# Backward of two attention blocks: every DMA on SyncE's queue, and a group's `wo` fetched head by head

## The chip, the cores and the metric

The kernel runs on one core of a Trainium2 chip. The metric is the device time of one execution in microseconds (us). The engines named below are TensorE (PE, with PEld for its weight loads), VectorE (DVE), ScalarE (ACT), GpSimd (POOL) and SyncE (SP). SyncE computes nothing here: its instruction stream is a queue of DMA issues with the semaphore waits that stand before them.

## What is computed

Two attention blocks, A and B, of the same shapes but with their own data, run forward, and then all gradients are formed for a given `grad_out`. There are 8 batches of 96 query tokens (768 rows), a model width of 640, 32 heads of width 128, and a cache of 512 keys per batch and head. Everything is bf16.

```python
q = (x @ wq) split into heads
p = softmax((q @ k_cache^T) * Dh**-0.5)
o = p @ v_cache
out = concat_heads(o) @ wo                      # for A and for B, side by side in out
# returned: out, and for both blocks dx, dk_cache, dv_cache, dwq, dwo
```

## The kernel before, in words

**Ticks.** The work is cut into items, one for each head and batch: 8 to a head, 512 in all. `build_block` gives every piece of an item, a head or a group a tick and a slot, and `Emitter.run` (L25) emits all pieces sorted by tick, then slot. Item *b* of head *h* starts at tick `tick0 + 8h + b`, and its stages follow at the ticks of `OFF` (L45): load at 0, transposes of K and V at 2, scores and exponential at 3, dV at 4, the output at 5, dP and dS at 6, dK and the transposition of dS at 7, dQ at 8. So in one tick TensorE does one stage of each of several items. The framework then schedules the emitted instructions and fixes for each engine, and for SyncE's queue, one static order. An instruction waits in that order for the semaphores of what it needs, and everything behind it on its engine waits too.

**One item on SyncE's queue.** `c_ld` (L235) loads K and V (128 KB each, 11 buffers of `K_sb` and 8 of `V_sb`); `c_s4` (L341) and `c_s7` (L407) store dV and dK (128 KB each, 6 buffers each). That is 32 issues for each head.

**One head.** `pA` (L174) loads the head's slice of `wq` as `wq_h` (one buffer, 640 runs of 256 bytes) and transposes by DMA its slice of `wo` into `woT_h` (one buffer); `pW` (L192) transposes a slice of `wq` into `wqT_h`; `pC` projects q and dO; `qA` (L410) transposes the finished `OT_h` and `dQT_h` by DMA into `Onat` and `dQnat` (one buffer each); `qB` (L419) forms dwo in two halves from `Onat` and stores it; `qD` (L437) forms dwq in three parts from `dQnat` and stores it. By `HK` (L46) `dQnat` is transposed at tick 16 after the head's first, and the matmuls that read it (L450) stand at ticks 19 to 21, three to five ticks later, which is in the stream of items of the head after the next.

**One group.** 8 heads are a group, and each block has 4. After a group's last item, `gU` (L471) sums the eight heads' products with `wo_r` (out) and with `wqT_h` (dx) in 12 units each, spread over 26 ticks (`GSPREAD`). These ticks hold more TensorE work, so they are longer. `gW` (L459) loads the whole group's `wo` into one tile `wo_r`, in a single DMA of 1280 KB.

**Which queue.** SyncE's queue has the item traffic, the DMA transposes, block A's x and g, the first `wq_h`, and block B's output rows. GpSimd issues the other `wq_h` loads, the stores of dwo and dwq, the `wo_r` loads, block A's output rows, block B's x and g in natural layout (L139) and block B's column chunks of g (L106). GpSimd also computes `P_sb` (L296) and `prod` (L350), in the same instruction stream as its DMA issues. Block B's x comes through five DMA transposes `xT` (L99) on SyncE's queue.

**Waits on SyncE's queue.** The DMAs of a queue share 8 completion semaphores in turn, and each issue waits for the landing of the DMA eight places before it, besides its own data or buffer.

Of the kernel before, what the change touches and what calls it, by code (L numbers as in the profile page):

```python
# [11 lines left out]
BF16 = mybir.dt.bfloat16  # L12
# [18 lines left out]
SL_LOAD = 0  # L31
# [10 lines left out]
SL_GRP = 95  # L42
SL_SETUP = 96

OFF = dict(ld=0, s1=2, s2=3, s3=3, s4=4, s5=5, s6=6, s7=7, s8=8)  # L45
# [3 lines left out]
GSPREAD = 26  # L49
# [3 lines left out]
def build_block(tc, em, tick0, blk, x, kc, vc, wq, wo, g_all, out_all, dx, dk, dv, dwq, dwo, ident, ones, pools, HG=8, first=True, groups=None):  # L53
    nc = tc.nc
    B, Sq, D = x.shape
# [8 lines left out]
    HG = min(HG, H)  # L64
    if groups is None:
        assert H % HG == 0
        groups = [HG] * (H // HG)
    assert sum(groups) == H and max(groups) <= HG
    NG = len(groups)
    GH0 = [sum(groups[:i]) for i in range(NG)]  # L70
# [8 lines left out]
    g_flat = g_all.rearrange("b s d -> (b s) d")[:, blk * D:(blk + 1) * D]  # L79
    out_flat = out_all.rearrange("b s d -> (b s) d")[:, blk * D:(blk + 1) * D]  # L80
    dx_flat = dx.rearrange("b s d -> (b s) d")
    wq_v = wq.rearrange("(c p) n -> p c n", p=128)
    dwq_v = dwq.rearrange("(c p) n -> p c n", p=128)

    const, ps, kvp, wk, hd, hst, grp = (pools[k] for k in ("const", "ps", "kvp", "wk", "hd", "hst", "grp"))

    def bank(shape, dt, name):
        return ps.tile(shape, dt, name=name, tag="bank")

    S = {}  # L90
    G = {}
    HS = pools["HS"]
    CS = pools["CS"]

# [7 lines left out]
    def setup_ld(c):  # L102
        def f():
            tmp = const.tile([128, TT, 128], BF16, name="ld_tmp", bufs=2)
            with nc.allow_non_contiguous_dma(reason="setup column chunk"):
                tc.keep_in_program_order(nc.gpsimd.dma_start(tmp[:], g_flat[:, c * 128:(c + 1) * 128].rearrange("(t p) d -> p t d", p=128)))  # L106
            S[("tmp", c)] = tmp
        return f

# [23 lines left out]
    def setup_nat(which_, t0=0, nt=TT):  # L133
        def f():
            key = "x_nat" if which_ == 0 else "g_nat"
            src_flat = x_flat if which_ == 0 else g_flat
            if t0 == 0:
                S[key] = const.tile([128, TT, D], BF16, name=key, bufs=1)
            (nc.sync if first else nc.gpsimd).dma_start(S[key][:, t0:t0 + nt, :],  # L139
                                                        src_flat[t0 * 128:(t0 + nt) * 128, :].rearrange("(t p) d -> p t d", p=128))  # L140
        return f

    def setup_acc():
        if NG > 1:
            S["out_acc"] = const.tile([128, TT, D], F32, name="out_acc", bufs=1)
            S["dx_acc"] = const.tile([128, TT, D], F32, name="dx_acc", bufs=1)
# [18 lines left out]
    def evac(eng, dst, src, sc=None):  # L165
        if eng == "act":
            nc.scalar.activation(dst, src, ACT.Identity, scale=(1.0 if sc is None else sc))
        else:
            if sc is None:
                nc.vector.tensor_copy(dst, src)  # L170
            else:
                nc.vector.tensor_scalar(dst, src, float(sc), None, op0=ALU.mult)

    def pA(h):  # L174
        def f():
            cols = slice(h * 128, (h + 1) * 128)
            wq_h = hd.tile([128, DC, 128], BF16, name="wq_h", bufs=1)
            with nc.allow_non_contiguous_dma(reason="per-head wq slice"):
                (nc.sync if first and h == 0 else nc.gpsimd).dma_start(wq_h[:], wq_v[:, :, cols])
            woT_h = hd.tile([128, DC, 128], BF16, name="woT_h", bufs=1)  # L180
            nc.sync.dma_start_transpose(woT_h[:], wo[cols, :])
            HS[(blk, h)] = dict(wq_h=wq_h, woT_h=woT_h)
        return f
# [235 lines left out]
    def qB(h, di):  # L419
        def f():  # L420
            st = HS[(blk, h)]
            Onat = st["Onat"]
            if "dwo_sb" not in st:
                st["dwo_sb"] = hd.tile([128, D], BF16, name="dwo_sb")
                st["dwo_n"] = 0
            dwo_sb = st["dwo_sb"]
            (c0, w) = dsplits[di]
            w_ps = bank([128, w], F32, "dwo_ps")
            for t in range(TT):
                nc.tensor.matmul(w_ps[:], Onat[:, t, :], S["g_nat"][:, t, c0:c0 + w], start=(t == 0), stop=(t == TT - 1))  # L430
            evac(EV["qB%d" % di], dwo_sb[:, c0:c0 + w], w_ps[:])
            st["dwo_n"] += 1
            if st["dwo_n"] == len(dsplits):
                nc.gpsimd.dma_start(dwo[h * 128:(h + 1) * 128, :], dwo_sb[:])
        return f

    def qD(h, c_lo, c_hi):  # L437
        def f():
            st = HS[(blk, h)]
            dQnat = st["dQnat"]  # L440
            if "dwq_sb" not in st:
                st["dwq_sb"] = hd.tile([128, DC, 128], BF16, name="dwq_sb")
                st["dwq_n"] = 0
            dwq_sb = st["dwq_sb"]
            ncn = c_hi - c_lo
            w_ps = bank([128, 4 * 128], F32, "dwq_ps")
            for ci in range(ncn):
                c = c_lo + ci
                for t in range(TT):
                    nc.tensor.matmul(w_ps[:, ci * 128:(ci + 1) * 128], S["x_nat"][:, t, c * 128:(c + 1) * 128], dQnat[:, t, :],  # L450
                                     start=(t == 0), stop=(t == TT - 1))
            evac("act" if ncn > 1 else "dve", dwq_sb[:, c_lo:c_hi, :].rearrange("p a b -> p (a b)"), w_ps[:, 0:ncn * 128])
            st["dwq_n"] += ncn
            if st["dwq_n"] == DC:
                with nc.allow_non_contiguous_dma(reason="per-head dwq slice"):
                    nc.gpsimd.dma_start(dwq_v[:, :, h * 128:(h + 1) * 128], dwq_sb[:])
        return f

    def gW(g):  # L459
        def f():  # L460
            wo_r = grp.tile([128, HG, D], BF16, name="wo_r", bufs=1)
            ld = nc.gpsimd.dma_start(wo_r[:, 0:groups[g], :], wo[GH0[g] * 128:(GH0[g] + groups[g]) * 128, :].rearrange("(h p) d -> p h d", p=128))
            tc.keep_in_program_order(ld)
            G[g] = dict(wo_r=wo_r)
            if g == 0:
                setup_acc()
        return f

# [2 lines left out]
    def gU(g, which, t, gi):  # L471
        def f():
            acc = S.get("out_acc" if which == 0 else "dx_acc")
            dst_flat = out_flat if which == 0 else dx_flat
            (c0, w) = gsplits[gi]
            o_ps = bank([128, w], F32, "o_ps")
            for hh in range(groups[g]):
                h = GH0[g] + hh
                src = HS[(blk, h)]["OT_h"] if which == 0 else HS[(blk, h)]["dQT_h"]
                rhs = G[g]["wo_r"][:, hh, c0:c0 + w] if which == 0 else HS[(blk, h)]["wqT_h"][:, c0:c0 + w]  # L480
                nc.tensor.matmul(o_ps[:], src[:, t * 128:(t + 1) * 128], rhs, start=(hh == 0), stop=(hh == groups[g] - 1))  # L481
            if NG == 1:
                ob = wk.tile([128, w], BF16, name="ob", bufs=4)
                evac(EV["gU"], ob[:], o_ps[:])
                nc.gpsimd.dma_start(dst_flat[t * 128:(t + 1) * 128, c0:c0 + w], ob[:])
            elif g == 0:
                evac(EV["gU"], acc[:, t, c0:c0 + w], o_ps[:])
            elif g < NG - 1:
                nc.vector.tensor_tensor(acc[:, t, c0:c0 + w], o_ps[:], acc[:, t, c0:c0 + w], op=ALU.add)
            else:  # L490
                ob = wk.tile([128, w], BF16, name="ob", bufs=4)
                nc.vector.tensor_tensor(ob[:], o_ps[:], acc[:, t, c0:c0 + w], op=ALU.add)
                (nc.gpsimd if first else nc.sync).dma_start(dst_flat[t * 128:(t + 1) * 128, c0:c0 + w], ob[:])
        return f

    NTS = len(tsplits)
# [2 lines left out]
    for g in range(NG):  # L499
        h0 = GH0[g]  # L500
        for hh in range(groups[g]):
            h = h0 + hh
# [32 lines left out]
            for (k_, c_lo, c_hi) in qd_parts:  # L535
                if c_lo < DC:
                    em.add(c0t + k_, SL_HEAD + 2, qD(h, c_lo, min(c_hi, DC)))
        cLg = tick0 + (h0 + groups[g] - 1) * B + B - 1
        em.add(cLg + OFF["s5"] - 2, SL_LOAD, gW(g))
        units = [(t, gi) for t in range(TT) for gi in range(len(gsplits))]  # L540
        for i, (t, gi) in enumerate(units):
            em.add(cLg + OFF["s5"] + 2 + (i * GSPREAD) // len(units), SL_GRP, gU(g, 0, t, gi))
# [116 lines left out]
```

## Time and profile before

| what | value |
|---|---|
| median of 3 runs | 1777.6 us (1771.38 to 1781.83) |
| profiled execution: its own time | 1778.72 us |
| profiled execution: span | 1776.9 us |
| granted TensorE clock, mean | 0.995 |
| busy share PE / PEld / DVE / ACT / POOL | 99 / 83 / 82 / 83 / 40 % |
| DMA time of SyncE's queue (q1), of 16 engines' span | 70.5 %, 319.82 MB |
| DMA time of GpSimd's queue (q0) | 8.8 %, 46.71 MB |
| DMA issues in the trace: SyncE / GpSimd | 2340 / 230 |

The span is the profiled part of that execution; 1.8 us of its own time lie around it. The profile is of one execution, so its parts are compared with 1778.72 us, and that time lies 1.1 us above the median of the three runs. In lines of the timeline the two first numbers are the start and the length in us; `SPq` marks an instruction of SyncE's queue, whose length is that of the issue and not that of the transfer. In lists of waits the three numbers are the total in us, how often, and the longest. Line numbers (L450) are those of the kernel before.

### The profile page before, as it was taken

Reading aid. Unit: us, or ns where it says so; the run is one execution under the profiler, and the core shown is the slowest. Engines: PE = TensorE matmul, PEld = TensorE weight load, DVE = VectorE, ACT = ScalarE, POOL = GpSimd, SP = SyncE. Lnnn points to the kernel's source line nnn. Section 1 sums busy time; section 2 is a strip of 40 time slices with the busy share of each in tenths; the row PEclk is TensorE's granted clock in tenths of the full one; section 3 lists DMA queues with packets and bytes.
Section 4 is the critical chain, followed back from the end, with each engine's and each line's share of the span. In section 5 each row is a group of like instructions: output and inputs, shape, how many; then the busy total and the mean of one; then the engine's idle time right before and its main releaser. Section 6 shows DMA issues by size and latency. Waiting matters only on the chain.

```text
span 1776.9 us, 65815 instructions
## 1 busy us (share of the span) xinstructions
PE 1752.8 (99%) x24538; PEld 1476.6 (83%) x24538; DVE 1449.4 (82%) x3106; ACT 1470.3 (83%) x4081; POOL 717.1 (40%) x1260
## 2 busy tenths in 40 slices
PE   8999899999999999999899999999999999999998
PEld 6888788888888888888788888888888888888886
DVE  7888766888878887788687888668987788878894
ACT  5999788899778987798777999789987799877992
POOL 2444433444334443345344444334443344433441
PEclk9999999999999999999899999999999999999999
DMA  8889975899858896689997799678896788867874
GB/s 212 220 221 221 240 191 167 206 217 237 210 168 214 217 245 186 178 209 223 236 254 188 211 222 248 186 178 208 221 245 183 182 219 225 238 179 174 222 215 128
DMA packets 508657, 370.73 MB, mean 209 GB/s; under 512 B 230000, under 2 KB 497136, under 8 KB 508336
## 3 DMA queue, kind: packets, MB, share of 16 engines
q1 hardware_dynamic: 493072, 319.82, 70.5%
q0 software_dynamic: 15264, 46.71, 8.8%
q8 instruction: 192, 3.15, 0.8%
q14 instruction: 129, 1.06, 0.2%
HBM read 160.10 MB, written 159.12 MB: 180 GB/s over the span
## 4 chain that ended last, share of the span: by engine, by line
PE 97%; DMA 2%; DVE 1%; issue 0%; ACT 0%; POOL 0%; SPq 0%; ACTq 0%; DVEq 0%; POOLq 0%
PE q_ps L215 12%; PE o_ps L481 12%; PE dK_ps L404 6%; PE dV_ps L338 6%; PE kvT_ps L249 6%; PE kvT_ps L251 6%; PE dP_ps L360 6%; PE S_ps L265 6%; PE dwq_ps L450 6%; PE dwo_ps L430 6%; PE dq_dst_ps L387 5%; PE optp_ps L321 5%; PE optp_ps L312 5%; PE dq_dst_ps L378 5%; PE n_ps L231 4%; DMA xT<-in_B_x_dram 1%
## 5 line engine op out<-in xcount | busy, mean ns | idle before, releaser
L296 POOL TENSOR_SCALAR P_sb<-E_sb,rinv 96x512 bf16<-96x512 bf16 x512 | 352.3, 688 | 680.6 <-DVE rinv L287 674.7
L277 ACT ACTIVATE E_sb<-S_ps,negm 96x512 bf16<-96x512 f32 x512 | 348.7, 681 | 152.1 <-DVE negm L267 151.4
L364 DVE SCALAR_TENSOR_TENSOR dS_sb<-dP_ps,dl_ps,P_sb 96x512 bf16<-96x512 f32 x512 | 384.7, 751 | 106.6 <-PE dl_ps L362 97.6
L267 DVE TENSOR_REDUCE negm<-S_ps 96x1 f32<-96x512 f32 x512 | 348.2, 680 | 56.7 <-PE S_ps L265 55.1
L253 DVE COPY KVT<-kvT_ps 128x1024 bf16<-128x1024 bf16 x512 | 348.5, 681 | 18.5 <-PE kvT_ps L251 6.3
L406 ACT ACTIVATE dK_sb<-dK_ps 128x512 bf16<-128x512 f32 x512 | 302.9, 592 | 51.9 <-PE dK_ps L404 48.5
L340 ACT ACTIVATE dV_sb<-dV_ps 128x512 bf16<-128x512 f32 x512 | 315.6, 616 | 0.0
L327 ACT ACTIVATE PT_sb<-optp_ps 128x384 bf16<-128x384 bf16 x512 | 254.3, 497 | 0.0
L350 POOL TENSOR_TENSOR prod<-OT_h,dOT_h 128x96 bf16<-128x96 bf16 x512 | 186.8, 365 | 106.4 <-ACT OT_h L324 87.4
L249 PE MATMUL kvT_ps<-ident,K_sb 128*128 128x128 bf16 x2048 | 198.4, 219 | 0.0
L251 PE MATMUL kvT_ps<-ident,V_sb 128*128 128x128 bf16 x2048 | 198.4, 219 | 0.0
L404 PE MATMUL dK_ps<-Qnat_h,dS_sb 96*128 96x128 bf16 x2048 | 198.4, 219 | 0.0
L338 PE MATMUL dV_ps<-dOnat_h,P_sb 96*128 96x128 bf16 x2048 | 198.1, 219 | 0.0
L265 PE MATMUL S_ps<-KVT,QT_h 128*96 128x512 bf16 x512 | 194.3, 380 | 1.2 <-DVE KVT L253 1.2
L360 PE MATMUL dP_ps<-KVT,dOT_h 128*96 128x512 bf16 x512 | 195.5, 382 | 0.0
L249 PEld LDWEIGHTS <-K_sb 128*128 128x128 bf16 x2048 | 152.1, 98 | 37.2 <-issue 2.0
L389 DVE COPY dST_sb<-dq_dst_ps 128x384 bf16<-128x384 bf16 x512 | 178.9, 349 | 2.1 <-PE dq_dst_ps L387 1.6
L321 PE MATMUL optp_ps<-ident,P_sb 96*128 96x96 bf16 x2048 | 171.9, 205 | 2.4 <-POOL P_sb L296 2.3
L387 PE MATMUL dq_dst_ps<-ident,dS_sb 96*128 96x96 bf16 x2048 | 172.5, 206 | 0.8 <-DVE dS_sb L364 0.4
L312 PE MATMUL optp_ps<-PT_sb,V_sb 128*128 128x96 bf16 x2048 | 172.5, 206 | 0.0
L378 PE MATMUL dq_dst_ps<-dST_sb,K_sb 128*128 128x96 bf16 x2048 | 171.1, 206 | 0.0
L450 PE MATMUL dwq_ps<-dQnat,x_nat 128*128 128x128 bf16 x1920 | 160.3, 220 | 5.0 <-DMA dQnat<-dQT_h 5.0
(71 smaller groups left out, 3560.3 us busy)
## 6 DMA issues: line engine op xcount, KB each, us to landing
out_dram<-dV_sb SPq DMA_DIRECT2D x512, 128.0 KB, 2.6
out_dram<-dK_sb SPq DMA_DIRECT2D x512, 128.0 KB, 2.6
K_sb<-in_A_k_cache_dram SPq DMA_DIRECT2D x256, 128.0 KB, 2.8
V_sb<-in_A_v_cache_dram SPq DMA_DIRECT2D x256, 128.0 KB, 2.7
K_sb<-in_B_k_cache_dram SPq DMA_DIRECT2D x256, 128.0 KB, 2.6
V_sb<-in_B_v_cache_dram SPq DMA_DIRECT2D x256, 128.0 KB, 2.6
out_dram<-dwo_sb POOLq DMA_DIRECT2D x64, 160.0 KB, 3.0
out_dram<-dwq_sb POOLq DMA_DIRECT2D x64, 160.0 KB, 3.2
```

Of the source, the lines that this page charges most:

```text
L249: nc.tensor.transpose(kvT_ps[:, c * 128:(c + 1) * 128], st["K_sb"][:, c, :], ident[:])
L251: nc.tensor.transpose(kvT_ps[:, Sk + c * 128:Sk + (c + 1) * 128], st["V_sb"][:, c, :], ident[:])
L253: nc.vector.tensor_copy(KVT[:], kvT_ps[:])
L267: nc.vector.tensor_reduce(negm[:], S_ps[:], axis=AX.X, op=ALU.max, negate=True)
L277: nc.scalar.activation(E_sb[:], st["S_ps"][:], ACT.Exp, bias=st["negm"][:], scale=1.0, accum_out=rowsum[:])
L296: nc.gpsimd.tensor_scalar(P_sb[:], st["E_sb"][:], st["rinv"][:], 0.0, op0=ALU.mult, op1=ALU.add)
L338: nc.tensor.matmul(dV_ps[:, c * 128:(c + 1) * 128], P_sb[:, c * 128:(c + 1) * 128], hs["dOnat_h"][:, b * 128:(b + 1) * 128], start=True, s ...
L340: nc.scalar.activation(dV_sb[:], dV_ps[:], ACT.Identity, scale=1.0)
L360: nc.tensor.matmul(dP_ps[:], hs["dOT_h"][:, tok], st["VT"], start=True, stop=True)
L364: nc.vector.scalar_tensor_tensor(dS_sb[:], dP_ps[:], dl_ps[:, 0:1], st["P_sb"][:], op0=ALU.subtract, op1=ALU.mult)
L404: nc.tensor.matmul(dK_ps[:, c * 128:(c + 1) * 128], dS_sb[:, c * 128:(c + 1) * 128], hs["Qnat_h"][:, b * 128:(b + 1) * 128], start=True, s ...
L406: nc.scalar.activation(dK_sb[:], dK_ps[:], ACT.Identity, scale=1.0)
```

## The change

Every `nc.gpsimd.dma_start` becomes `nc.sync.dma_start`. The single load of a group's `wo` becomes eight loads of 160 KB, one for each head, into eight tiles of their own. They stand in the last 31 ticks of the group's 64 (from tick 33 of the group on, about one every four ticks), where the single load stood two ticks before the group's last item was through its stage 5. The matmuls are the same and read the head's tile.

```diff
-                tc.keep_in_program_order(nc.gpsimd.dma_start(tmp[:], g_flat[:, c * 128:(c + 1) * 128]...
+                tc.keep_in_program_order(nc.sync.dma_start(tmp[:], g_flat[:, c * 128:(c + 1) * 128]...
...
-            (nc.sync if first else nc.gpsimd).dma_start(S[key][:, t0:t0 + nt, :],
+            nc.sync.dma_start(S[key][:, t0:t0 + nt, :],
...
-                (nc.sync if first and h == 0 else nc.gpsimd).dma_start(wq_h[:], wq_v[:, :, cols])
+                nc.sync.dma_start(wq_h[:], wq_v[:, :, cols])
...
-                nc.gpsimd.dma_start(dwo[h * 128:(h + 1) * 128, :], dwo_sb[:])
+                nc.sync.dma_start(dwo[h * 128:(h + 1) * 128, :], dwo_sb[:])
...
-                    nc.gpsimd.dma_start(dwq_v[:, :, h * 128:(h + 1) * 128], dwq_sb[:])
+                    nc.sync.dma_start(dwq_v[:, :, h * 128:(h + 1) * 128], dwq_sb[:])
...
-    def gW(g):
+    def gW(g, hh):
         def f():
-            wo_r = grp.tile([128, HG, D], BF16, name="wo_r", bufs=1)
-            ld = nc.gpsimd.dma_start(wo_r[:, 0:groups[g], :], wo[GH0[g] * 128:(GH0[g] + groups[g]) * 128, :]...
-            tc.keep_in_program_order(ld)
-            G[g] = dict(wo_r=wo_r)
-            if g == 0:
+            h = GH0[g] + hh
+            wo_r = grp.tile([128, D], BF16, name="wo_r", bufs=HG)
+            tc.keep_in_program_order(nc.sync.dma_start(wo_r[:], wo[h * 128:(h + 1) * 128, :]))
+            HS[(blk, h)]["wo_r"] = wo_r
+            if g == 0 and hh == 0:
                 setup_acc()
...
-                (nc.gpsimd if first else nc.sync).dma_start(dst_flat[t * 128:(t + 1) * 128, c0:c0 + w], ob[:])
+                nc.sync.dma_start(dst_flat[t * 128:(t + 1) * 128, c0:c0 + w], ob[:])
...
-        em.add(cLg + OFF["s5"] - 2, SL_LOAD, gW(g))
+        lead = 2 + OFF["s5"] + GSPREAD
+        for hh in range(groups[g]):
+            em.add(tick0 + h0 * B + lead + ((groups[g] * B - lead) * hh) // groups[g], SL_GRP + 2, gW(g, hh))
```

The order that the scheduler fixes for TensorE, VectorE and ScalarE is the same as before, instruction for instruction. GpSimd's order loses its 230 DMA issues. SyncE's queue goes from 2340 DMA issues to 2626.

More of the change, by code (lines that the diff above doesn't have):

```diff
@@ L90, in build_block @@
     S = {}
-    G = {}
     HS = pools["HS"]
@@ L105, in f @@
             with nc.allow_non_contiguous_dma(reason="setup column chunk"):
-                tc.keep_in_program_order(nc.gpsimd.dma_start(tmp[:], g_flat[:, c * 128:(c + 1) * 128].rearrange("(t p) d -> p t d", p=128)))
+                tc.keep_in_program_order(nc.sync.dma_start(tmp[:], g_flat[:, c * 128:(c + 1) * 128].rearrange("(t p) d -> p t d", p=128)))
             S[("tmp", c)] = tmp
@@ L455, in f @@
                 with nc.allow_non_contiguous_dma(reason="per-head dwq slice"):
-                    nc.gpsimd.dma_start(dwq_v[:, :, h * 128:(h + 1) * 128], dwq_sb[:])
+                    nc.sync.dma_start(dwq_v[:, :, h * 128:(h + 1) * 128], dwq_sb[:])
         return f
-    def gW(g):
+    def gW(g, hh):
         def f():
-            wo_r = grp.tile([128, HG, D], BF16, name="wo_r", bufs=1)
-            ld = nc.gpsimd.dma_start(wo_r[:, 0:groups[g], :], wo[GH0[g] * 128:(GH0[g] + groups[g]) * 128, :].rearrange("(h p) d -> p h d", p=128))
-            tc.keep_in_program_order(ld)
-            G[g] = dict(wo_r=wo_r)
-            if g == 0:
+            h = GH0[g] + hh
[3 more added lines that the diff above has]
+            if g == 0 and hh == 0:
                 setup_acc()
@@ L479, in f @@
                 src = HS[(blk, h)]["OT_h"] if which == 0 else HS[(blk, h)]["dQT_h"]
-                rhs = G[g]["wo_r"][:, hh, c0:c0 + w] if which == 0 else HS[(blk, h)]["wqT_h"][:, c0:c0 + w]
+                rhs = HS[(blk, h)]["wo_r"][:, c0:c0 + w] if which == 0 else HS[(blk, h)]["wqT_h"][:, c0:c0 + w]
                 nc.tensor.matmul(o_ps[:], src[:, t * 128:(t + 1) * 128], rhs, start=(hh == 0), stop=(hh == groups[g] - 1))
@@ L484, in f @@
                 evac(EV["gU"], ob[:], o_ps[:])
-                nc.gpsimd.dma_start(dst_flat[t * 128:(t + 1) * 128, c0:c0 + w], ob[:])
+                nc.sync.dma_start(dst_flat[t * 128:(t + 1) * 128, c0:c0 + w], ob[:])
             elif g == 0:
@@ L492, in f @@
                 nc.vector.tensor_tensor(ob[:], o_ps[:], acc[:, t, c0:c0 + w], op=ALU.add)
-                (nc.gpsimd if first else nc.sync).dma_start(dst_flat[t * 128:(t + 1) * 128, c0:c0 + w], ob[:])
+                nc.sync.dma_start(dst_flat[t * 128:(t + 1) * 128, c0:c0 + w], ob[:])
         return f
```

## Prediction

> **What bounds the kernel.** I read the page's first two parts, then the waits, then TensorE's few idle places in the windows view, and last the timeline of SyncE's queue. TensorE sets the end:
>
> ```profile
> PE 1752.8 (99%) x24538; PEld 1476.6 (83%) x24538; DVE 1449.4 (82%) x3106; ACT 1470.3 (83%) x4081; POOL 717.1 (40%) x1260
> ...
> DMA  8889975899858896689997799678896788867874
> ```
>
> TensorE is idle in few places, and nearly all of that is DMA:
>
> ```profile
> POOL P_sb L296 <- DVE rinv L287: 674.7, 389, 8.2
> ...
> PE q_ps L215 <- DMA xT<-in_B_x_dram: 6.3, 3, 2.7
> ...
> PE dwq_ps L450 <- DMA dQnat<-dQT_h: 5.0, 1, 5.0
> ...
> PE tp_ps L129 <- DMA x_nat<-in_A_x_dram: 4.5, 2, 3.8
> ```
>
> The 674.7 us are GpSimd's own spare time; TensorE waited 2.3 us for `P_sb` in all. So GpSimd's 230 issues cost nothing now, and taking them away frees an engine that nobody waits for. The two stalls in mid-run cost more than their length, since the granted clock falls after them (columns: window, length, busy us of PE, PEld, DVE, ACT, POOL, then PEclk, DMA share, GB/s):
>
> ```profile
> 190.00:204.00 14.00, 14.00 (x210) 11.99 (x207) 12.54 (x28) 13.13 (x38) 7.32 (x13) 1.00 1.03 199
> 204.00:214.00 10.00, 4.96 (x53) 4.44 (x51) 2.77 (x6) 3.00 (x11) 1.30 (x3) 0.66 1.03 301
> ...
> 846.00:859.00 13.00, 7.23 (x55) 5.47 (x55) 3.09 (x7) 3.38 (x9) 2.00 (x4) 0.61 0.97 252
> ```
>
> A clock of 0.66 over 10 us loses 3.4 us beside the wait of 5.0 us; 0.61 over 13 us loses 5.1 us beside 6.3 us.
>
> Now SyncE's queue, between two groups of units (start, length of the issue):
>
> ```profile
> 343.43 0.43 SPq L407 DMA_DIRECT2D out_dram<-dK_sb  x1
> 343.95 0.39 SPq L341 DMA_DIRECT2D out_dram<-dV_sb  x1
> 344.44 0.43 SPq L239 DMA_DIRECT2D K_sb<-in_A_k_cache_dram  x1
> 344.96 0.39 SPq L240 DMA_DIRECT2D V_sb<-in_A_v_cache_dram  x1
> 345.44 0.47 SPq L407 DMA_DIRECT2D out_dram<-dK_sb  x1
> 346.01 1.66 SPq L416 DMA_TRANSPOSE dQnat<-dQT_h  x1
> 347.76 0.54 SPq L341 DMA_DIRECT2D out_dram<-dV_sb  x1
> 348.39 0.38 SPq L239 DMA_DIRECT2D K_sb<-in_A_k_cache_dram  x1
> ```
>
> Each issue starts 0.1 us after the last one ended: **the queue is full**. A head is 36 issues, 32 direct and 4 transposes. From the K load at 340.2 us to the one a head later it takes 24.9 us, and the next two heads 24.5 and 25.4 us, while TensorE needs 23.84 us for a head without units. So the queue falls behind by about 1 us a head. During a group's units a head lasts 27 to 32 us, the queue has pauses of some 30 us in all, and it catches up. Whoever is served late shows it first at `dQnat`: the time from its landing to its first matmul (L450) is 8.8, 6.5, 4.6, 4.1, 2.1 us for heads 10 to 14 (of 0 to 63).
>
> **What the change does, part by part.** TensorE's, VectorE's and ScalarE's orders stay the same, so only waits can move the time.
>
> *The burst goes.* One transpose of 64 was hit by the 1280 KB load:
>
> ```profile
> 198.49 0.95 POOL L462 DMA_DIRECT2D wo_r<-in_A_wo_dram  x1
> ...
> L416 SPq DMA_TRANSPOSE dQnat<-dQT_h x64: 1217/1277/2718, 51.3 to 1745.6; - x64
> ...
> DMA to landing us min/median/max: 2.5/3.8/10.4
> ```
>
> It was issued 0.3 us after that load and took 10.4 us instead of 3.85: 6.5 us come back. The other seven loads were issued after their transpose, which landed in 2.5 to 4.8 us, so nothing comes back there.
>
> *286 issues come to SyncE's queue* (230 less the 8 big loads, plus 64 small ones). Price: a direct issue of 128 runs takes 0.38 us and 0.10 us to the next, 0.48 us. A `wq_h` issue (640 runs) stands on this queue once, at the start, with 0.47 us: 0.56 us; I give the dwq store, of the same shape, the same. The mean, 0.52 us, is my price. From below: 0.43 us (0.33 us, an issue after a pause, and 0.10). From above: behind that one `wq_h` the next transpose took 2.79 us against 1.24 us; if half the new issues each held up the queue by 1.5 us more, the mean is 1.3 us. I take the near row, because six other loads of 256 runs stood in front of that transpose too.
>
> *Where they stand.* In heads with units three a head come in, in heads without units five (`wq_h`, dwo, dwq and two of `wo_r`, whose eight loads fall into the last 31 ticks of the group, where the queue is full). Counted in the new order, from the queue's last pause to the last `dQnat` before a group's units (heads 6, 14, 22, 29, 38, 46, 54, 62), against the time to spare of that `dQnat`:
>
> | group | added | x 0.52 us | to spare | new wait of TensorE |
> |---|---|---|---|---|
> | 1 | 27 | 14.0 | -5.0 + 6.5 | 12.5 |
> | 2 | 19 | 9.9 | 2.1 | 7.8 |
> | 3 | 19 | 9.9 | 4.8 | 5.1 |
> | 4 (setup of B) | 14 | 7.3 | 4.9 | 2.4 |
> | 5 | 25 | 13.0 | 3.2 | 9.8 |
> | 6 | 19 | 9.9 | 2.9 | 7.0 |
> | 7 | 19 | 9.9 | 6.3 | 3.6 |
> | 8 | 18 | 9.4 | 7.9 | 1.5 |
>
> Sum 49.7 us, less the 5.0 us already waited: **+44.7 us**. The waits come in pieces at the `dQnat` of two to four heads; behind L450 in TensorE's order stands all of the next items' work, so each piece delays everything. In the units' heads the queue has some 30 us of pauses against 8 us of new issues and up to 13 us of lateness, so that is made good there and each group starts anew. The K and V loads have 1 to 3 us more to spare at most in those heads and would be the next to be late.
>
> *Setup of B.* `xT` waits already now. Before its last chunk 17 issues are added (8.8 us, 2.4 of them already counted), and behind it come two more `ld_tmp` (1.0 us): **+7.4 us**.
>
> *Block A's output rows, B's x and g in natural layout*: 26 issues in heads with units, hidden by the queue's pauses there; without that cover 26 x 0.52 = 13.5 us.
>
> *Clock.* In the two rows above a stall costs 0.7 to 0.8 us of clock per us waited. Taken on all 52 us this would be +37; but a TensorE at half clock also gives the queue that time, so it replaces the next wait and only the last of a stretch counts. Ends: -8.5 (the two old losses vanish) and +28 (37 less 8.5, which are in the span). I take **+5**, nearer to none, as the pieces are short.
>
> **Sum:** 1778.7 + 44.7 + 7.4 + 5 = **1836 us**, 57 us over the profiled execution and 3.3% over the median of 1777.6 us.
>
> **Two rules that speak against this.** The queue of rows above is full at 0.48 us an issue. The Trainium skill, "DMA: Bandwidth & Descriptors", section "Issuing engines are not separate DMA queues", says that DMAs issued from several engines run on the same 16 DMA engines, and spreading them saves only issue time, "usually small relative to the DMA itself". By that rule the sum is without the issue terms, the profiled execution less the stall at 204 us and its clock loss, near 1770 us. Here an issue is short against its landing (0.4 against 2.6 us), but 36 of them fill a head.
>
> On the clock: gaps of 2.74, 2.04 and 1.52 us within 7.2 us led to the 0.61 row. The skill's "TensorE: Matmul & The Clock Gate", section "Part 1: The HAM clock gate", has the clock halve after an idle window of about 3.4 us; by that alone no piece under 3.4 us costs clock, and the clock term would be near -8.5 instead of +5.
>
> **Rivals.**
> 1. *The queue has room, the burst was the problem* (ends on the other side). Then the stall at 204 us goes with its clock loss, 5.0 + 3.4 us: 1770 us; if `xT` also lands in time without GpSimd's traffic, 11.4 us more: 1759 us. For it: the worst stall is the burst's. Against it: no pause in four heads of SyncE's queue. It decides if 19 issues cost less than 2.1 to 6.3 us, 0.1 to 0.3 us each.
> 2. *Partly absorbed*: at the low price of 0.43 us the eight waits are 35.5 us, setup 5, clock -8.5: 35.5 - 5.0 + 5 - 8.5 = +27, 1806 us; if loads also land faster, down to 1787.
> 3. *The 256-byte runs are dear.* At 1.3 us an issue, 19 issues are 25 us and the eight waits 174 us: with 20 us in the setup 1973 us at the far end; at 0.8 us they are 94 us, setup 12: 1778.7 + 94 - 5.0 + 12 + 5 = 1885 us. For it: the 2.79 us, and the DMA engines are already at 0.95 to 1.03 in these heads. Against: one row only, at the start.
>
> **Chances.** Forecast (1806 to 1865) 0.55; rival 3 (above 1865) 0.17; rival 2's lower part (1787 to 1806) 0.11; no change 0.08; rival 1 below 1769 us 0.09. What this measurement can tell from no change is about 0.5%, 1768.7 to 1786.5 us. So faster 0.09, same 0.08, slower 0.83. The range 1788 to 1892 us leaves out those two and a few hundredths above.
>
> **What would show it.** Right: waits `PE dwq_ps L450 <- DMA dQnat` of 30 to 70 us in 15 to 30 pieces, at the ends of groups; SyncE's heads without units at 26.5 to 27.5 us; no pauses there; rows of PEclk below 1.00 near the stalls; GpSimd waiting for nothing new. Wrong: SyncE's issues of `wq_h` or dwq far from 0.47 us, transposes behind them over 2 us, the K and V loads as the main releaser of TensorE, or `dQnat` landing in under 3 us throughout.

## The result, and the profile after

| what | before | after |
|---|---|---|
| median of the runs beside each other | 1778.8 us (4 runs) | 1833.53 us (4 runs, 1827.56 to 1837.91) |
| ratio to before | | 1.0312, 95% interval 1.0268 to 1.0356 |
| profiled execution: its own time / span | 1778.72 / 1776.9 us | 1827.56 / 1825.7 us |
| TensorE idle between its first and its last matmul | 17.0 us | 52.6 us |
| SyncE's queue, a head without units | 24.54 us for 36 issues | 27.30 us for 41 issues |

The change costs 3.1%; forecast were 1836 us. The last row is the mean over the 22 heads that have no units in them and exactly these numbers of issues, their time taken from one head's first K load to the next. In the lines below the numbers of the lines are one lower than before (L450 is now L449), since the change takes a line out near the top.

First the page of after, its lines of the engines, of the DMA engines' busy tenths and of SyncE's queue:

```profile
PE 1766.2 (97%) x24538; PEld 1481.0 (81%) x24538; DVE 1449.9 (79%) x3106; ACT 1469.6 (80%) x4081; POOL 539.9 (30%) x1030
...
DMA  7888886889867887778887877977778777887774
...
q1 hardware_dynamic: 603760, 366.53, 77.6%
```

GpSimd is busy 177 us less and nobody gains by it. The DMA engines are no fuller than before: the bytes are the same, and one queue now has nearly all of them. Next, what TensorE waited for (total, times, longest):

```profile
PE dwq_ps L449 <- DMA dQnat<-dQT_h: 23.6, 16, 3.3
PE kvT_ps L248 <- DMA K_sb<-in_A_k_cache_dram: 7.4, 5, 3.7
PE kvT_ps L250 <- DMA V_sb<-in_A_v_cache_dram: 5.8, 10, 1.5
PE kvT_ps L250 <- DMA V_sb<-in_B_v_cache_dram: 5.8, 9, 1.3
...
PE tp_ps L116 <- DMA ld_tmp<-in_grad_out_dram: 4.5, 1, 4.5
...
PE kvT_ps L248 <- DMA K_sb<-in_B_k_cache_dram: 0.6, 1, 0.6
```

The `dQnat` wait that before had once, for 5.0 us, is there 16 times. K and V, for which TensorE never waited, take 19.6 us in 25 pieces. The `xT` row of before (6.3 us) is gone, and `ld_tmp` has come in its place. So the readers of four different DMAs wait a little each, and what these four have in common is the queue.

The windows view, for the two places shown of before and for four new ones (busy us of PE, PEld, DVE, ACT, POOL, then PEclk, DMA share, GB/s):

```profile
190.00:204.00 14.00, 12.82 (x201) 11.02 (x199) 11.04 (x26) 11.79 (x35) 4.21 (x9) 1.00 0.86 226
204.00:214.00 10.00, 10.00 (x138) 8.21 (x137) 9.05 (x20) 9.37 (x28) 4.19 (x8) 1.00 0.75 204
133.00:139.00 6.00, 3.19 (x52) 2.76 (x50) 2.96 (x7) 3.00 (x9) 1.06 (x2) 1.00 1.03 154
139.00:147.00 8.00, 7.30 (x82) 6.54 (x79) 4.08 (x9) 3.85 (x11) 1.06 (x2) 0.57 0.90 255
859.00:866.00 7.00, 4.32 (x49) 3.93 (x50) 2.09 (x5) 1.86 (x6) 1.06 (x2) 0.77 0.76 185
866.00:880.00 14.00, 9.51 (x101) 7.68 (x100) 5.61 (x13) 5.19 (x15) 1.60 (x3) 0.75 0.93 229
```

The burst's place, 204 to 214 us, is clean: full clock, TensorE busy throughout. At 133 to 139 us TensorE waits 2.81 us for one `dQnat`, and at 139 to 147 us its clock is 0.57. In the setup of B two such pairs follow each other.

Last the timeline of SyncE's queue (start, length of the issue), at the place where before was shown:

```profile
347.07 0.57 SPq L462 DMA_DIRECT2D wo_r<-in_A_wo_dram  x1
347.74 0.38 SPq L238 DMA_DIRECT2D K_sb<-in_A_k_cache_dram  x1
348.22 0.38 SPq L239 DMA_DIRECT2D V_sb<-in_A_v_cache_dram  x1
348.69 0.38 SPq L406 DMA_DIRECT2D out_dram<-dK_sb  x1
349.16 0.38 SPq L340 DMA_DIRECT2D out_dram<-dV_sb  x1
349.63 0.38 SPq L455 DMA_DIRECT2D out_dram<-dwq_sb  x1
350.11 0.55 SPq L238 DMA_DIRECT2D K_sb<-in_A_k_cache_dram  x1
```

The newcomers stand between the item traffic, still with 0.1 us between one issue and the next. The dwq store of 640 runs takes 0.38 us, like a K load of 128 runs, but the K load behind it takes 0.55 us. Over the whole trace, an issue of the item traffic straight behind `wq_h` or dwq (short runs) takes 0.54 to 0.55 us at the median, and behind dwo or `wo_r` 0.38 to 0.40; the `wo_r` load takes 0.57 us itself, the dwo store 0.41. With this and the 0.09 us to the next issue, the prices are about 0.64 (`wq_h`), 0.65 (dwq), 0.51 (dwo) and 0.67 us (`wo_r`). Per added issue the head is (27.30 - 24.54) / 5 = 0.55 us longer. The pauses of the queue, over the time of the heads, fall from 229 to 104 us; in the 22 heads without units they are 0.3 us a head, before and after. A K or V load lands in 2.5 to 2.8 us by the page, as before (2.6 to 2.8), and `dQnat` in 3.4 us at the median (before 3.85).

**Where the time went.** The span grew by 48.8 us: TensorE's idle time by 35.6, its busy time by 13.4, and the ends before its first and behind its last matmul are 0.2 us shorter. Of the 13.4, the stretches at half clock give 3.4 us (half their length: 11.95 against 8.53 us). That leaves 10 us.

### The profile page after: what moved, and what is told of

The parts are those of the page before. It is cut to its first block, busy times and chain, and to the rows that moved or that the text cites. A ratio compares the mean times of both kernels' runs of the same rounds, so it can differ in the third digit from the quotient of the medians.

```text
span 1825.7 us, 65832 instructions
## 1 busy us (share of the span) xinstructions
PE 1766.2 (97%) x24538; PEld 1481.0 (81%) x24538; DVE 1449.9 (79%) x3106; ACT 1469.6 (80%) x4081; POOL 539.9 (30%) x1030
## 3 DMA queue, kind: packets, MB, share of 16 engines
q8 instruction: 192, 3.15, 0.8%
## 4 chain that ended last, share of the span: by engine, by line
PE 91%; DMA 7%; ACT 1%; DVE 1%; SPq 0%; issue 0%; POOL 0%; ACTq 0%; DVEq 0%; POOLq 0%
PE q_ps L214 12%; PE o_ps L480 11%; PE kvT_ps L250 6%; PE dK_ps L403 6%; PE dV_ps L337 6%; PE kvT_ps L248 6%; PE dP_ps L359 6%; PE S_ps L264 6%; PE dwq_ps L449 6%; PE dwo_ps L429 5%; PE dq_dst_ps L386 5%; PE optp_ps L311 5%; PE optp_ps L320 5%; PE dq_dst_ps L377 5%; PE n_ps L230 3%; DMA V_sb<-in_A_v_cache_dram 2%
## 5 line engine op out<-in xcount | busy, mean ns | idle before, releaser
L250 PE MATMUL kvT_ps<-ident,V_sb 128*128 128x128 bf16 x2048 | 199.0, 220 | 11.7 <-DMA V_sb<-in_A_v_cache_dram 5.8
L248 PEld LDWEIGHTS <-K_sb 128*128 128x128 bf16 x2048 | 151.9, 98 | 46.7 <-DMA K_sb<-in_A_k_cache_dram 8.9
L449 PE MATMUL dwq_ps<-dQnat,x_nat 128*128 128x128 bf16 x1920 | 161.6, 221 | 24.2 <-DMA dQnat<-dQT_h 23.6
```

The costliest lines, as they stand in the source:

```text
L248: nc.tensor.transpose(kvT_ps[:, c * 128:(c + 1) * 128], st["K_sb"][:, c, :], ident[:])
L250: nc.tensor.transpose(kvT_ps[:, Sk + c * 128:Sk + (c + 1) * 128], st["V_sb"][:, c, :], ident[:])
```

## The experiments

The theory: SyncE's queue is full in heads without units, each further issue makes the queue some 0.5 us later there, and TensorE waits for whatever has the least time to spare. Its rivals: the 256-byte runs are dear; `dQnat` alone is late; the bytes that moved into the queue are in the way, not the issues.

**1. The load of wo by head alone.** The kernel before, with `wo` by head as in the change, but on GpSimd's queue, and all the other DMAs where they were (SyncE's queue has its 2340 issues as before):

```diff
...
+            wo_r = grp.tile([128, D], BF16, name="wo_r", bufs=HG)
+            tc.keep_in_program_order(nc.gpsimd.dma_start(wo_r[:], wo[h * 128:(h + 1) * 128, :]))
...
```

> The kernel before, with only the second half of the change: wo comes by head into eight tiles, but on GpSimd's queue, and all other DMAs stay where they were. SyncE's order is unchanged. Theory (the change loses by filling SyncE's queue, and the wo part alone is a small gain): the 10.4 us transpose at 199 us lands in about 4 us, the wait of 5.0 us at L450 and its 3.4 us of clock go, and the time is about 8 us below before, near 1770 us. Rival (wo by head is itself what costs): slower than before, up to the 1833 us of the changed kernel.

1769.42 us, ratio 0.9949 (0.9935 to 0.9962). Its list of TensorE's waits:

```profile
PE q_ps L214 <- DMA xT<-in_B_x_dram: 5.9, 3, 3.0
...
PE dwq_ps L449 <- DMA dQnat<-dQT_h: 0.6, 2, 0.5
```

The stall behind the burst is gone, as is its stretch of half clock, and `xT` is as late as it was. This part of the change is a gain of 0.5%. The rest of it, which moves the DMAs, then costs 1.0312 / 0.9949, 3.6%.

**2. More issues, the same bytes.** The kernel before, with the V load of every second item cut into two loads of 64 partitions, 256 more issues on SyncE's queue:

```diff
-            nc.sync.dma_start(V_sb[:], vc[b, h].rearrange("(p c) d -> p c d", c=KC))
+            vsrc = vc[b, h].rearrange("(p c) d -> p c d", c=KC)
+            if b % 2 == 0:
+                nc.sync.dma_start(V_sb[0:64], vsrc[0:64])
+                nc.sync.dma_start(V_sb[64:128], vsrc[64:128])
+            else:
+                nc.sync.dma_start(V_sb[:], vsrc)
```

> The kernel before, with the V load of every second item issued as two halves of 64 partitions: 256 more issues on SyncE's queue, the same bytes and runs, nothing moved from GpSimd, wo still in one load. Theory (the number of issues is the price, 0.52 us each): 16 more issues in each stretch without units, 28 in the first; by the same working as in the prediction about 39 us of waits before a group's units, some 6 us in the setup of B and a few us of clock, so 1815 to 1830 us; SyncE's heads without units take 26 to 27 us and TensorE waits for dQnat and for K and V. Rival (the moved transfers themselves cost: their 256-byte runs, or the loss of a second queue): within 10 us of before.

1882.6 us, ratio 1.0586 (1.0564 to 1.0607): the direction was right, the size was missed by over 50 us. The timeline of SyncE's queue shows why (L242 and L243 are the halves, L245 a whole V load):

```profile
344.30 0.53 SPq L239 DMA_DIRECT2D K_sb<-in_A_k_cache_dram  x1
344.92 0.48 SPq L242 DMA_DIRECT2D V_sb<-in_A_v_cache_dram  x1
345.49 0.54 SPq L412 DMA_DIRECT2D out_dram<-dK_sb  x1
346.07 0.47 SPq L243 DMA_DIRECT2D V_sb<-in_A_v_cache_dram  x1
...
348.44 0.40 SPq L245 DMA_DIRECT2D V_sb<-in_A_v_cache_dram  x1
348.93 0.38 SPq L412 DMA_DIRECT2D out_dram<-dK_sb  x1
```

A half takes 0.47 us, more than the whole load (0.40), and the issue behind a half takes 0.54 us instead of 0.38. A head without units is 28.03 us for 40 issues, 0.87 us an added issue. So an issue's price isn't one number: it depends on its shape and on its neighbours. That more issues with the same bytes and the same runs cost time is shown; the price of the change's own issues can't be read from this kernel.

**3. Issues with next to no bytes.** To come nearer to it, the kernel of experiment 1 with a load of 8 KB, of 128 partitions, on SyncE's queue beside each of the four DMAs of a head whose change of queue it leaves out (`wq_h`, dwo, dwq, `wo_r`); and the same beside two of the four only (`wq_h`, `wo_r`):

```diff
+    def tiny(h):
+        z = hd.tile([128, 32], BF16, name="tiny", bufs=3)
+        tc.keep_in_program_order(nc.sync.dma_start(z[:], wo[h * 128:(h + 1) * 128, 0:32]))
...
+            tiny(h)
...
```

> The kernel before with wo by head on GpSimd, and beside each of the four loads and stores of a head that GpSimd issues (wq_h, dwo, dwq, wo_r) one more load on SyncE's queue, of 128 runs of 64 bytes (8 KB) that nobody reads: 256 issues with next to no bytes. Theory (SyncE's queue lacks issue time, the bytes don't matter): the loss of the changed kernel comes back nearly whole, 1805 to 1830 us, with waits for dQnat, K and V and SyncE's heads without units at 26.5 to 27.5 us. Rival (the moved DMAs' bytes stand ahead of the item traffic in the same queue, the issues don't matter): 1767 to 1775 us.

> As the kernel with four small loads a head, with two (beside wq_h and wo_r): 128 issues. Theory (a wait of TensorE is lateness less time to spare): clearly less than half the loss of four a head, 1772 to 1785 us. Rival (each issue on a full queue costs its time at the end): half of that loss, 1787 to 1800 us.

With four a head: 1816.35 us, ratio 1.0246 (1.0197 to 1.0294). From 0.9949 that is 3.0%, of the 3.6% that the moved DMAs cost. A head without units is 27.07 us for 41 issues, 0.46 us an added issue over the 24.75 us of experiment 1. The waits of TensorE (lines are 5 or 6 higher here):

```profile
PE kvT_ps L255 <- DMA V_sb<-in_A_v_cache_dram: 10.5, 8, 2.8
PE kvT_ps L253 <- DMA K_sb<-in_A_k_cache_dram: 9.5, 8, 3.0
PE q_ps L219 <- DMA xT<-in_B_x_dram: 6.3, 3, 3.0
...
PE kvT_ps L253 <- DMA K_sb<-in_B_k_cache_dram: 3.1, 4, 1.4
PE kvT_ps L255 <- DMA V_sb<-in_B_v_cache_dram: 3.0, 6, 0.7
PE dwq_ps L455 <- DMA dQnat<-dQT_h: 2.4, 6, 1.1
```

Mostly the same readers wait, in another division, though 2 MB were added to the queue where the change moves 46.7 MB there. **The issues are most of the cost.** With experiment 2, which adds issues and neither bytes nor runs, this settles it. The 0.6% left can be the bytes, the 30 issues that this kernel has fewer than the changed one, or the price: a small load has about 0.54 us, the moved DMAs 0.51 to 0.67. In groups 2, 3 and 5 to 8 TensorE waits 14.6 us for DMAs here and 27.5 us in the changed kernel, so there the small loads give only half.

With two a head: 1788.13 us, ratio 1.0065 (1.0034 to 1.0096), 39% of the loss of four a head. The theory had said under 1785, its rival (in proportion) from 1787: the number fell to the rival. The halving was my slip: of the five small loads in a head without units three remain, since the `wo_r` loads come two to a head there. In proportion to three of five, 60% would have been lost, and 39% were. So the forecast time was missed, but time to spare did cover part of the lateness: in groups 2, 3 and 5 to 8 TensorE waits 5.7 us for DMAs, against 14.6 with four a head.

**4. Either half of the moved DMAs back to GpSimd.** The changed kernel with the short runs back (`wq_h`, dwq: 256 bytes), or with the long ones back (dwo, `wo_r`: 1280 bytes):

```diff
-                    nc.sync.dma_start(dwq_v[:, :, h * 128:(h + 1) * 128], dwq_sb[:])
+                    nc.gpsimd.dma_start(dwq_v[:, :, h * 128:(h + 1) * 128], dwq_sb[:])
```

> The changed kernel, with the DMAs of 256-byte runs (wq_h loads and dwq stores, 127 of them) back on GpSimd's queue; dwo, wo_r and the rest stay on SyncE's (2499 issues). Theory (issues count, whatever their runs; waits at the end of a group are the issues added in the stretch before it less the time to spare): 12 added issues in a usual stretch instead of 19, so about 16 us of waits at dQnat and beside it, 4 us in the setup and 3 us of clock: 1797 to 1808 us, some half of the loss left. Rival (the short runs on the hardware queue are what costs): 1775 to 1785 us.

> The changed kernel, with the DMAs of 1280-byte runs (dwo stores and wo_r loads by head, 128 of them) back on GpSimd's queue; wq_h, dwq and the rest stay on SyncE's (2498 issues, as many as in the kernel with the short runs back). Theory (issues count, and where they stand): 7 added issues in a usual stretch, since the wo_r loads stood just there, so about 6 us of waits, 2 us in the setup and 2 us of clock: 1782 to 1793 us, faster than the kernel with the short runs back. Rival (short runs cost): 1815 to 1830 us, slower than it.

Short runs back: 1785.05 us, ratio 1.0052 (1.0037 to 1.0067); the forecast of 1797 to 1808 was missed by 12 us, and the number stands at the edge of its rival's (1785). Long runs back: 1788.27 us, ratio 1.0083 (1.0066 to 1.01), inside its forecast and far from the rival's 1815. Of the change's 3.1% the one gives back five sixths and the other three quarters, more than the whole together, as where a queue goes from just enough to too little. The waits of TensorE show it: in groups 2, 3 and 5 to 8 they are 2.4 us for DMAs in the first kernel and 1.0 in the second, against 27.5 in the changed one. Two or three added issues a head are nearly covered there by the time to spare; five are not. What is left stands in group 1 and in the setup of B (16.4 and 17.3 us, 11.7 before), and the longest wait of either list is there:

```profile
PE tp_ps L116 <- DMA ld_tmp<-in_grad_out_dram: 9.7, 1, 9.7
```

```profile
PE tp_ps L116 <- DMA ld_tmp<-in_grad_out_dram: 7.2, 1, 7.2
```

Short runs can't be the cause by themselves, since without the long ones nearly as much is gone. By my count the first should have been the slower of the two (three of five issues remain in a head without units, against two). The heads do follow the count (26.15 us for 39 issues, 25.75 for 38), the times do not; why not stays open.

**5. Readers of dQnat later.** The changed kernel with the dwq matmuls two ticks later, which gives `dQnat` some 6 us more (the engines' orders move with it):

```diff
-HK = dict(..., qD=[(19, 0, 2), (20, 2, 4), (21, 4, 5)])
+HK = dict(..., qD=[(21, 0, 2), (22, 2, 4), (23, 4, 5)])
```

> The changed kernel, with the dwq matmuls that read dQnat two ticks later (21, 22, 23 instead of 19, 20, 21), which gives each dQnat some 6 us more to spare; the scheduler's orders move with it. Theory (SyncE's queue is short of time as a whole, and dQnat is only the first to show it): the waits at dQnat (23.6 us) nearly go, those for K and V loads (19.6 us) grow by most of it, and the time stays within 10 us of the changed kernel, 1822 to 1838 us. Rival (the late transposes are the cause and K and V only follow from them): 18 us or more come back, 1795 to 1815 us.

1838.75 us, ratio 1.0356 (1.0329 to 1.0384), 0.8 us above the range stated and no faster than the changed kernel. Its waits:

```profile
PE tp_ps L116 <- DMA ld_tmp<-in_grad_out_dram: 14.4, 1, 14.4
PE kvT_ps L250 <- DMA V_sb<-in_B_v_cache_dram: 12.6, 11, 2.1
PE kvT_ps L250 <- DMA V_sb<-in_A_v_cache_dram: 10.4, 9, 2.4
PE kvT_ps L248 <- DMA K_sb<-in_A_k_cache_dram: 5.2, 4, 1.9
```

No `dQnat` any more, and no time gained: TensorE waits for V and `ld_tmp` instead (K and V 28.5 us instead of 19.6, `ld_tmp` 14.4 instead of 4.5). The row with the most us in a list of waits names the reader that came first, not the cause.

**6. Another engine's queue for the moved DMAs.** The changed kernel with `wq_h`, `wo_r`, dwo and dwq issued by ScalarE:

```diff
-                nc.sync.dma_start(dwo[h * 128:(h + 1) * 128, :], dwo_sb[:])
+                nc.scalar.dma_start(dwo[h * 128:(h + 1) * 128, :], dwo_sb[:])
```

> The changed kernel, with the wq_h and wo_r loads and the dwo and dwq stores issued by ScalarE instead of SyncE: the same transfers in hardware queues and the same runs, but only 31 issues more on SyncE's queue than before (2371). Theory (SyncE's issue time is the price): no stall at dQnat and none at 204 us, 1768 to 1785 us, with ScalarE's own 255 issues hidden in its 17% of idle time; if they delay its evacuations, some us more. Rival (the hardware path with short runs loads the DMA engines and delays all landings): near the changed kernel, 1820 to 1835 us.

1812.83 us, ratio 1.0189 (1.0169 to 1.0209): missed by 28 us. Its waits:

```profile
PE dwo_ps L429 <- ACT E_sb L276: 12.4, 12, 2.3
PE S_ps L264 <- ACT dK_sb L405: 9.5, 26, 1.5
...
PE kvT_ps L248 <- ACT dQT_h L392: 4.9, 7, 1.6
```

SyncE's queue is relieved (25.3 us a head with 36 issues, with pauses of 2.1 us a head), K, V and `dQnat` are in time (0.7 us in all), but now TensorE waits for ScalarE, 31 us in all. Its issues take 0.35 to 0.4 us each and stand in the stream that empties TensorE's banks. The same transfers with the same runs are there, which speaks against them as the reason why K, V and `dQnat` were late; but the slower TensorE gives the queue some of its pauses, so this alone wouldn't show it. Off SyncE isn't enough; the issues have to go to an engine for which nobody waits.

**7. wo in one piece on SyncE's queue.** The changed kernel with one load of 1280 KB a group, at the place of the last of the eight:

```diff
+            if hh == groups[g] - 1:
+                wo_r = grp.tile([128, HG, D], BF16, name="wo_r", bufs=1)
+                tc.keep_in_program_order(nc.sync.dma_start(wo_r[:, 0:groups[g], :], wo[GH0[g] * 128:...
```

> The changed kernel, with a group's wo in one load of 1280 KB on SyncE's queue instead of eight of 160 KB (2570 issues instead of 2626): 8 added issues in a usual stretch instead of 19. Theory: fewer issues where the queue is full, about 14 us of waits by the working of the prediction, of which 5 were there before; the burst may delay a transpose again and cost 5 to 10 us in a group or two: 1790 to 1806 us. Rival (eight small loads are the good part of the change everywhere): 1833 us or slower.

1850.24 us, ratio 1.043 (1.0396 to 1.0464), missed by 44 us and on the other side of the changed kernel, with 56 issues fewer than it. The waits, and the window of the worst place:

```profile
PE kvT_ps L248 <- DMA K_sb<-in_A_k_cache_dram: 19.7, 3, 7.3
PE kvT_ps L248 <- DMA K_sb<-in_B_k_cache_dram: 15.4, 3, 5.9
```

```profile
205.00:212.00 7.00, 0.09 (x2) 0.01 (x1) 0.54 (x2) 1.10 (x3) 0.00 (x0) 0.76 1.18 304
```

```profile
201.65 0.57 SPq L463 DMA_DIRECT2D wo_r<-in_A_wo_dram  x1
...
205.69 0.91 SPq L238 DMA_DIRECT2D K_sb<-in_A_k_cache_dram  x1
206.69 0.58 SPq L239 DMA_DIRECT2D V_sb<-in_A_v_cache_dram  x1
208.98 0.34 SPq L406 DMA_DIRECT2D out_dram<-dK_sb  x1
```

The big load is issued at 201.65 us and lands 7.3 us later. The next K load is issued at 205.69 us, already late, and lands after 6.3 us instead of 2.6; all engines all but stand still meanwhile. The queue itself stops too: the dK store at 208.98 us is the issue eight places behind the big load, and it starts 1.7 us after the issue before it has ended, just when the big load has landed. Behind seven of the eight big loads the queue stops so, for 1.6 to 2.9 us. I had counted issues only. A large DMA ahead in the queue holds up the landing of those behind it and, through the semaphores in turn, their issue, and it does so at the end of the group, where nothing is to spare. So here, other than in experiment 3, bytes count: it is a piece of 1280 KB that hurts, not 46.7 MB that come mostly in pieces of 160 KB.

**8. A better version.** Experiment 1 left `xT` as the one wait in mid-run. Its five transposes were asked one a tick; first all five in one tick (`tick0 - 9`), then two a tick:

```diff
-            em.add(tick0 - 9 + c, SL_SETUP, setup_xbar(c))
+            em.add(tick0 - 9 + c // 2, SL_SETUP, setup_xbar(c))
```

> The first kernel of this call, with the five DMA transposes of block B's x asked for in one tick instead of one tick after the other. Theory: their last chunk lands before its first matmul, so the waits of 6.3 us at L215 and 5.1 us of clock go as well as the 8 us of the first kernel: 1755 to 1762 us. Rival (SyncE's queue is full there, so five transposes in a row only move the wait to K, V or dQnat): 1766 to 1775 us.

> The kernel before with wo by head on GpSimd, and xT's transpositions asked two to a tick from the same tick on. Theory: the five together pushed K's loads too late (4.8 us of waiting for K_sb), one a tick brings xT too late (5.9 us); two a tick spread them enough that neither waits over 1 us: 1755 to 1764 us. Rival: the queue needs the same time for the five whatever their spacing, so xT or K waits 3 to 6 us still, with a stretch of half clock behind it: 1766 to 1771 us.

All in one tick: 1768.67 us, ratio 0.9942 (0.993 to 0.9955), no gain over experiment 1, as the rival had it: `xT` is in time, and TensorE waits 4.8 us for a K load behind it. Two a tick: 1764.43 us, ratio 0.9918 (0.9898 to 0.9937), the lowest time of all kernels here. What TensorE waits for in it:

```profile
PE tp_ps L128 <- DMA x_nat<-in_A_x_dram: 5.3, 2, 3.7
PE kvT_ps L248 <- DMA K_sb<-in_A_k_cache_dram: 3.2, 1, 3.2
```

The time is 0.4 us above the theory's range and below the rival's, and the theory's condition (no wait over 1 us) wasn't met: TensorE waits 3.2 us for a K load, with 3.41 us at half clock behind it, as the rival had it. The intervals of the two spacings overlap a little, so the gain of the one over the other isn't certain; that both beat the kernel before is.

## Why the prediction was right, and which of its terms were not

**The queue is full: right.** Experiments 2 and 3 slow the kernel by issues alone. The heads without units were to be 26.5 to 27.5 us; they are 27.3, with 0.3 us of pauses.

**The price of 0.52 us: right for the change's issues on average** (0.55 measured, 0.46 for the small loads, 0.61 in experiment 4 with the long runs back). Rival 3 fell with its 0.8 to 1.3 us an issue, though not altogether: `wq_h` and dwq issue in 0.39 and 0.41 us at the median, dwo, with long runs, in 0.41, but the issue behind the short runs is some 0.15 us longer. That makes 0.64 and 0.65 us, no more than the 0.67 us of `wo_r`, whose runs are long. The 2.79 us transpose that spoke for rival 3 was a single one: the 64 transposes `woT_h` take 1.23 us at the median, before as after. Experiment 2 shows that the same term would have been wrong by two thirds for half-height loads.

**The table of waits: mis-sized.** By group, all DMA waits of TensorE in after, added from the trace, beside the table:

| group | said | measured | of it K and V |
|---|---|---|---|
| 1 | 12.5 | 9.2 | 3.9 |
| 2 | 7.8 | 2.3 | 1.0 |
| 3 | 5.1 | 3.5 | 1.9 |
| 4, with the setup of B | 2.4, and the setup 6.7 + 7.4 | 10.9 | 6.4 |
| 5 | 9.8 | 9.7 | 2.2 |
| 6 | 7.0 | 3.8 | 1.9 |
| 7 | 3.6 | 5.3 | 2.3 |
| 8 | 1.5 | 2.9 | 0 |

`dQnat` was said to wait 49.7 us (30 to 70 as a sign to look for) and waited 23.6, in 16 pieces. K and V, "the next to be late", waited 19.6 us, nearly as much, which the sum had at nothing. One wait replaces the other: what TensorE has waited for a V load, the `dQnat` behind it in the queue need not be waited for. The table took one reader for all, and came near the sum of them for that reason. Groups 1, 2 and 6 waited 3.3, 5.5 and 3.2 us less than said; which of the time to spare was left out there stays open. Of the signs that the prediction named, the one for `dQnat` (30 us and more) was not met, and the one against it, K and V as the main releaser, nearly was.

**Made good in the units' heads: right.** The queue pauses 104 us in all, nobody waits for the moved DMAs of these heads, and after a group's last DMA wait TensorE has none for 152 to 195 us, into the end of the next group: each group starts anew.

**The setup of B: too high by 3 us, and wrong in the reader.** +7.4 us was said, with `xT` later and `ld_tmp` behind it. Waits in the setup went from 6.7 us to 10.9, +4.2. `xT` no longer waits, since K loads (1.99 and 3.7 us, at 848.7 and 857.7 us) and `ld_tmp` (4.5) hold TensorE up before it comes to read `xT`.

**The burst: right.** Its stall at 204 us is gone, and experiment 1 has that gain by itself (9 us, its clock loss included). Rival 1 held this to be all that the change does; it is true of that part, and wrong for the rest, which costs seven times as much.

**The clock: +5 said, +3.4 measured.** The losses moved: 6.83 and 10.24 us at half clock in two places before, 24 us in five pieces of 3.4 to 6.8 us after. The Trainium skill, "TensorE: Matmul & The Clock Gate", section "Part 1: The HAM clock gate", would by its idle window of about 3.4 us have given only the stretches behind the waits of 3.7 and 4.5 us in the setup. The trace also shows stretches of 6.83 and 3.41 us at half clock behind waits of 2.81, 2.56 and 3.26 us, each the longest among shorter ones. Here the measurement decides; waits up to 2.0 us left no such stretch.

The traces show more. In each of the 13 kernels all drops of the clock lie on one grid of 3.413 us, and each stretch at half clock is one to four cells of it long. Take the cells at full clock of all 13 traces (without the first 12 and the last 8 us) and the share of each in which TensorE was busy. Under 0.40, half clock followed 34 times of 34; from 0.40 to 0.48, 14 times of 17; above 0.48, none of 6643 times. So what counted was the busy share of a cell and not the length of one wait: the wait of 2.81 us fell almost whole into one cell and left 0.27 of it busy, and the cells before the drops behind 2.56 and 3.26 us were busy for 0.45 and 0.38. The wait of 2.0 us (at 1569 us) left 0.52.

**A term left out: about 10 us of TensorE's busy time.** The prediction took the waits as TensorE's idle time and its busy time as fixed. The busy time grew by 10 us more than the clock explains. A matmul lasts 0.22 us in the records, and in a stream the next one starts some 0.06 us behind it, so a stall should cost 0.16 us more than the idle time that the profile shows. Read matmul by matmul (the two traces have the same 24538 in the same order), this comes out. Outside the stretches at half clock there are 43 more pieces of idle time after than before; at these places the time from one matmul's start to the next one's grew by 44.1 us and the idle time by 37.1 us, which leaves 7.0 us, 0.16 us each. Pauses too short to show as idle time give another 1.7 us, and 4.7 us lie in the stretches at half clock, together the 13.4. So it was still the waits that moved the time, and each of them costs 0.16 us more than the list of waits says.

That the total of 1836 us came so close to 1833.53 is in part luck. The waits, forecast 16 us too long in all (49.7 and 14.1 against 47.6 us), stood in for these 10 us. What remains, 8.4 us over the profiled execution of 1827.56 us, shrinks to 2.5 against the median, since that execution is the fastest of the four.

**The rule on issuing engines.** The Trainium skill, "DMA: Bandwidth & Descriptors", section "Issuing engines are not separate DMA queues", calls the saving in issue time "usually small relative to the DMA itself". One issue is small here too (0.4 us, against 2.6 us to the landing). But where the queue is full the issues add up, and experiment 3 measures what they cost: 3.0%, with 2 MB more on 371 MB. The weighing in the prediction went the right way.

## What to carry to other kernels

Before DMAs are moved to another engine's queue, add up that queue's issues over the stretch where it has no pauses, against the time of the bounding engine for the same work; where the queue is within a few per cent of it, the issues beyond the time to spare are paid at the end, even with next to no bytes. Then look for the readers with little time to spare, all of them: relieving the one that shows up in the list of waits hands the wait to the next. And keep large loads out of the queue that feeds the inner loop: by pieces, from an engine that nobody waits for, the same `wo` was a gain, in one piece on the busy queue a loss.

## What was not expected of the hardware

- A load of 64 partitions takes longer to issue than one of 128 (0.47 against 0.40 us), and makes the next issue longer too (0.54 against 0.38): two halves cost 0.87 us more than one whole in a full queue (experiment 2). Behind a DMA of 256-byte runs the next issue is longer too (0.54 to 0.55 us, in the changed kernel).
- Behind a load of 1280 KB in the same queue a K load landed in 6.3 us instead of 2.6, and the issue eight places behind it waited 1.7 us for its landing (experiment 7), while 46.7 MB more, mostly in pieces of 160 KB, left the landings as they were (2.5 to 2.8 us).
- Waits of 2.6 to 3.3 us among shorter ones were followed by half clock for 3.4 to 6.8 us: what counted was a cell of a 3.413 us grid in which TensorE was busy for less than 0.40 (always) to 0.48 (mostly) of the time.
- Some 190 issues of SyncE in the kernel before are about 1 us longer than their like (a dV store of 1.20 us stands in after at 344.61). In the trace most of them end 1.3 to 2.5 us behind the start of one of the 192 packets of 16 KB of the instruction queue (the page's `q8 instruction: 192, 3.15, 0.8%`). That the one causes the other wasn't tried; if so, it takes some 170 us of SyncE's time, which no kernel here won back.
